# Projecting four tiles of x inside the gaps of a recurrent loop, with less room for staging, in a memory-augmented transformer with a SwiGLU gate

## The chip, the cores and the metric

The kernel runs on one core of one Trainium2 chip. The metric is the device time of one execution in microseconds (us). Times are medians of several executions. On one core the runs of one kernel differ by a few tenths of a per cent, so each experiment was timed in rounds together with the kernel before, on the same chip.

The engines have short names in the profile: PE is TensorE, PEld its weight loads, DVE is VectorE, ACT is ScalarE, POOL is GpSimd, SP is SyncE. PEclk is the clock that TensorE was granted, as a share of full speed. A number such as L354 is a line of the program of that kernel; the lines of the changed kernel are shifted against those of the kernel before.

## The reference

The forward part, cut to what matters. The kernel also computes the gradients of all nine inputs; that part is untouched.

```python
xn = layernorm(x)                          # x: (1, 2048, 640) bf16
mem = mem0                                 # (1, 8, 640)
for s in range(64):                        # segments of 32 tokens, each needs the memory of the last
    h = concat([mem, xn[:, 32*s:32*s+32]])
    q, k, v = h@Wq, h@Wk, h@Wv             # 32 heads of 128
    p = softmax(where(mask, q@k.T * 128**-0.5, -1e9))
    o = (p@v) @ Wo
    mem, out_s = o[:, :8], o[:, 8:]
g = silu( (silu(xn@w1) * (xn@w3)) @ w2 )   # SwiGLU, F = 1728
out = x + concat(out_s) * g
```

Only the 8 memory rows are recurrent. The 2048 rows of x can be projected at any time before their segment needs them.

## The kernel before

The forward part runs in this order: layer norm; SwiGLU; the turning (transposing) of the SwiGLU weights for the backward pass; the projection of the first rows of x, which also turns Wq, Wk, Wv and Wo; then the loop of 64 steps. A step is a chain: project the 8 memory rows, scores, softmax, product with v, product with Wo, next step. The other work of the loop is put into named gaps of this chain (W0, W1, W2, G1 to G6, in that order). That work is the attention of the x rows, one tile of 96 rows for every three steps, cut into eight units of four heads. Two of three steps take three units, the third takes two.

The up-front projection of 672 rows, the first seven tiles:

```python
units = wT_A_units(k, Wq, Wk_, Wv, Wo)     # 136 units: turn a piece of a weight, copy it out, store it
# pools: b0s (staging) with 3 buffers
for wi, (W, dst) in enumerate(((Wv, ...), (Wk_, ...), (Wq, ...))):
    for xt in range(6):                    # 6 x 112 rows
        for cg in range(4):
            st = stp.tile([112, 1024], BF16, name="b0st", tag="b0st")
            for b in range(2):
                ...                        # 5 matmuls 128x112 by 128x512 into pb
                k.copy(st[:, b*512:(b+1)*512], pb[:], eng='vs'[b])
            nc.sync.dma_start(dst[...], st[:])
            ...                            # then a few weight-turning units
```

The other 15 tiles cost no time of their own: 24 rows of them ride in each step, in free columns of the chain's own projection. In the gaps G2 to G5 stand seven warming matmuls of 128x512, whose results nobody reads:

```python
WARM = dict(G2=2, G3=1, G4=2, G5=2)
def gap(g):
    FILL(g, t, at, kbatch)                 # the x rows' work of this gap
    for i in range(WARM.get(g, 0)):
        nc.tensor.matmul((bA if g == "G4" else bB)[:], k.ident[:], Wq[:, 0, 0:512], start=True, stop=True)
```

The product of the x rows with v, in the gaps W0, W1 and W2, is copied to `xoT` on ScalarE and stored to DRAM as `OTX`, and ScalarE has the chain's own copies behind it:

```python
def pv(tl, qd, q=nc.gpsimd):
    ...
    ot = fl.tile([P, 4, 4, 24], BF16, name="xoT", tag="xoT", bufs=2)
    nc.scalar.copy(ot[:]..., pt[:]...)
    nc.scalar.dma_start(k.OTX[4*tl:4*tl+4, :, 4*qd:4*qd+4, :]..., ot[:]...)
```

Of the kernel before, what the change touches and what calls it, by code (L numbers as in the profile page):

```python
# [40 lines left out]
class K:  # L41
# [110 lines left out]
    def setup_dram(self):  # L152
        tc = self.tc
        S, D, T, H, F = self.S, self.D, self.T, self.H, self.F
        HD = self.HD
        dp = self.ctx.enter_context(tc.tile_pool(name="scratch", bufs=1, space=bass.MemoryType.DRAM))
        self.dp = dp
        mk = lambda name, shape, dt=BF16: dp.tile(list(shape), dt, name=name, uniquify=False)
        self.XN = mk("XN", (S, D))
        self.XNT = mk("XNT", (D, S))  # L160
        self.SLT = mk("SLT", (F, S))
        self.DUT = mk("DUT", (F, S))
        self.HB = mk("HB", (S, F))
        self.DZ = mk("DZ", (S, D))
        self.GB = mk("GB", (S, D))
        self.GS = mk("GS", (S, D))
        self.GST = mk("GST", (D, S))

        self.NR = S + 8 * T
        self.GXA = mk("GXA", (self.NR, D))  # L170
        self.HRO = mk("HRO", (self.NR, D))

        self.OT0 = 7
        self.NO = 4 * ((T - 1 - self.OT0) // 4)
        self.OTX = mk("OTX", (self.NO, P, H, 24))
        self.FS = mk("FS", (T, 64, 320))
        self.SR = mk("SR", (S, D))
        self.GWO = mk("GWO", (self.NR, D))


        self.QVS = mk("QVS", (T // 4, 4, 32, 4, 2, 1024))
        self.KS = mk("KS", (T // 4, 4, 32, 4, 1024))
        self.GOS = mk("GOS", (T // 4, 4, 32, 4, 1024))
        self.QM = mk("QM", (T, 8, HD))
        self.NB0 = 672
        self.QVX = mk("QVX", (self.NB0, 2, HD))
        self.KX = mk("KX", (self.NB0, HD))
        self.GB0 = 1344
        self.GX0 = mk("GX0", (S - self.GB0, HD))
        self.OR = mk("OR", (self.NTL * 120, HD))  # L190
        self.PR, self.DSR, self.VTD = [], [], []
        self.GXP = mk("GXP", (self.NTL, P, 8, 3, 2, 32), F32)
        for tl in range(self.NTL):
            n = self.geo(tl)[3]
            self.PR.append(mk(f"PR{tl}", (n, H, n)))
            self.DSR.append(mk(f"DSR{tl}", (n, H, n)))
            ns, nm = self.geo(tl)[0:2]
            self.VTD.append(mk(f"VTD{tl}", (P, ns, H, 40)))
        self.PM = mk("PM", (T, P, 80))
        self.WQT = mk("WQT", (HD, D))  # L200
        self.WKT = mk("WKT", (HD, D))
        self.WVT = mk("WVT", (HD, D))
        self.WOT = mk("WOT", (D, HD))
        self.W1T = mk("W1T", (F, D))
        self.W3T = mk("W3T", (F, D))
        self.W2T = mk("W2T", (D, F))
# [18 lines left out]
    def tok_src(self, x0, nx, w, c0, c1):  # L225
        if x0 + nx <= self.NB0:
            X0 = self.KX[:, c0:c1] if w == "k" else self.QVX[:, :, c0:c1] if w == "qv" else self.QVX[:, "qv".index(w), c0:c1]
            return [(0, nx, X0[x0:x0 + nx])]
        b, r = divmod(x0 - self.NB0, 96)
        assert r + nx <= 96  # L230
        return [(0, nx, self.blk_src(w, b, r, r + nx, c0, c1))]
# [174 lines left out]
def phase3_Afwd(k, W4, Wv):  # L406
    nc, tc = k.nc, k.tc
    D, DC, S, H, HD, T = k.D, k.DC, k.S, k.H, k.HD, k.T
    Wk_ = W4.tile([P, DC, HD], BF16, name="Wk", tag="w1")
# [4 lines left out]
    with tc.tile_pool(name="b0", bufs=1) as io, tc.tile_pool(name="b0s", bufs=3) as stp, \  # L414
# [5 lines left out]
        nc.sync.dma_start(Wk_[:], k.A_Wk.rearrange("(dc p) h e -> p dc (h e)", p=P))  # L420
        for wi, (W, dst) in enumerate(((Wv, k.QVX[:, 1]), (Wk_, k.KX[:, :]), (Wq, k.QVX[:, 0]))):
            for xt in range(6):
                x0 = 112 * xt
                if xt == 4 and wi == 0:
                    nc.scalar.dma_start(Wq[:], k.A_Wq.rearrange("(dc p) h e -> p dc (h e)", p=P))
                if xt == 4 and wi == 1:
                    nc.scalar.dma_start(Wo[:], k.A_Wo.rearrange("h e d -> e h d"))
                for cg in range(4):
                    st = stp.tile([112, 1024], BF16, name="b0st", tag="b0st")
                    for b in range(2):  # L430
                        c0 = cg * 1024 + b * 512
                        pb = ps.tile([112, 512], F32, name="b0pb", tag="b0pb")
                        for dc in range(DC):
                            nc.tensor.matmul(pb[:], xs[:, dc, x0:x0 + 112], W[:, dc, c0:c0 + 512],
                                             start=(dc == 0), stop=(dc == DC - 1))
                        k.copy(st[:, b * 512:(b + 1) * 512], pb[:], eng='vs'[b])
                    nc.sync.dma_start(dst[x0:x0 + 112, cg * 1024:(cg + 1) * 1024], st[:])
                    nu = ((wi * 24 + 4 * xt + cg + 1) * len(units)) // 72
# [4 lines left out]
    with tc.tile_pool(name="ast", bufs=1) as st, tc.tile_pool(name="achain", bufs=1) as ch, \  # L443
# [19 lines left out]
        rides = {}  # L463
        WARM = dict(G2=2, G3=1, G4=2, G5=2)

        def ride_ld(t):
            x0 = k.NB0 + 24 * t
            b, sub = t // 4, t % 4
            if sub == 0 and x0 < S:
# [19 lines left out]
        def ride(t):  # L489
            b, sub = t // 4, t % 4  # L490
            if k.NB0 + 96 * b >= S:
                return
# [3 lines left out]
        def chain(t, gap):  # L496
# [31 lines left out]
            qmT = ch.tile([P, H, 8], BF16, name="qmT", tag="qmT")  # L528
# [15 lines left out]
            sTm = ch.tile([40, 2, P], BF16, name="sTm", tag="sTm")  # L544
# [11 lines left out]
            sb = ch.tile([P, 2, 40], F32, name="msb", tag="msb")  # L556
# [14 lines left out]
            PTm = ch.tile([104, 8, 16], BF16, name="PTm", tag="PTm")  # L571
# [123 lines left out]
        def pv(tl, qd, q=nc.gpsimd):  # L695
# [3 lines left out]
            if 4 * tl < k.NO:  # L699
# [3 lines left out]
                ot = fl.tile([P, 4, 4, 24], BF16, name="xoT", tag="xoT", bufs=2)  # L703
# [25 lines left out]
        def gap_of(t):  # L729
# [5 lines left out]
            def gap(g):  # L735
                FILL(g, t, at, kbatch)
                m = len(batch.get(t, ()))
# [76 lines left out]
def phase3b_out(k, Wo, W0, W4):  # L814
# [8 lines left out]
    for (nm_, src, tag) in (("v", k.WVT, "w1"), ("k", k.WKT, "w2")):  # L823
        WT[nm_] = W4.tile([P, H, D], BF16, name=f"W{nm_}T", tag=tag)
# [738 lines left out]
def emit_wT_B(k: K, w1s, w3s, w2s, ps, ps_tag):  # L1563
    nc, tc = k.nc, k.tc
    D, DC, F, FC = k.D, k.DC, k.F, k.FC
    fszs = [min(P, F - fc * P) for fc in range(FC)]
    gi = 0
    with tc.tile_pool(name="wTB_st", bufs=4) as stp:
        for (nat, dstT) in ((w1s, k.W1T), (w3s, k.W3T)):
            for fc in range(FC):  # L1570
                fsz = fszs[fc]
                pt = ps.tile([P, DC, P], BF16, name="wTpt1", tag=ps_tag[gi % len(ps_tag)])
                for dc in range(DC):
                    nc.tensor.transpose(pt[0:fsz, dc, :], nat[:, dc, fc * P:fc * P + fsz], k.ident[:])
                st = stp.tile([P, DC, P], BF16, name="wTst1", tag="wTst1")
                k.copy(st[0:fsz], pt[0:fsz], eng=('v' if gi % 2 == 0 else 's'))
                gi += 1
                nc.sync.dma_start(dstT[fc * P:fc * P + fsz, :].rearrange("p (dc q) -> p dc q", q=P), st[0:fsz])
        for dc in range(DC):
            for fg in range(0, FC, 8):  # L1580
                nfc = min(8, FC - fg)
                pt = ps.tile([P, 8, P], BF16, name="wTpt2", tag=ps_tag[gi % len(ps_tag)])
                for i in range(nfc):
                    fc = fg + i
                    fsz = fszs[fc]
                    nc.tensor.transpose(pt[:, i, 0:fsz], w2s[0:fsz, fc, dc * P:(dc + 1) * P], k.ident[0:fsz, 0:fsz])
                st = stp.tile([P, 8, P], BF16, name="wTst2", tag="wTst8")
                nfull = sum(1 for i in range(nfc) if fszs[fg + i] == P)
                if nfull > 0:
                    k.copy(st[:, 0:nfull, :], pt[:, 0:nfull, :], eng=('v' if gi % 2 == 0 else 's'))  # L1590
                    gi += 1
                    nc.sync.dma_start(k.W2T[dc * P:(dc + 1) * P, fg * P:(fg + nfull) * P].rearrange("p (g q) -> p g q", q=P), st[:, 0:nfull, :])
                for i in range(nfull, nfc):
                    fc = fg + i
                    fsz = fszs[fc]
                    k.copy(st[:, i, 0:fsz], pt[:, i, 0:fsz], eng='s')
                    nc.sync.dma_start(k.W2T[dc * P:(dc + 1) * P, fc * P:fc * P + fsz], st[:, i, 0:fsz])


# [36 lines left out]
def phase2_Bfwd(k: K, Wv):  # L1636
# [5 lines left out]
    with tc.tile_pool(name="bw", bufs=1) as wp, tc.tile_pool(name="bio", bufs=2) as io, \  # L1642
            tc.tile_pool(name="bwork", bufs=2) as wk, tc.tile_pool(name="bps", bufs=2, space=bass.MemoryType.PSUM) as ps, \
# [10 lines left out]
        k.x_rows(k.HRO, k.XN, nc.gpsimd)  # L1654
        for blk in range(NBLK):
            b0 = blk * BLK
# [27 lines left out]
            for ti in range(BLK // P):  # L1684
# [33 lines left out]
                hb_tok = wk.tile([P, F], BF16, name="hb_tok", tag="hb_tok")  # L1718
# [4 lines left out]
        emit_wT_B(k, w1s, w3s, w2s, ps1, ("pht", "pz"))  # L1723
# [142 lines left out]
def kernel(  # L1866
# [35 lines left out]
    with tc.tile_pool(name="W0", bufs=1) as W0:  # L1902
        Wv = W0.tile([P, k.DC, k.HD], BF16, name="Wv", tag="w0")
        phase2_Bfwd(k, Wv)
        with tc.tile_pool(name="W4", bufs=1) as W4:
            Wo = phase3_Afwd(k, W4, Wv)
# [40 lines left out]
```

## Time and profile before

The time is 5646.7 us (median of three runs, 5643.7 to 5655.1). Times below are from the start of the profiled run, which took 5660.5 us.

| stretch | us | what holds it |
|---|---|---|
| layer norm and SwiGLU, to its last matmul | 0 to 312.5 | TensorE and the evictions |
| turns of the SwiGLU weights | 312.5 to 378.4 | evictions waiting for stores |
| up-front projection, with 136 weight-turning units | 378.4 to 593.3 | TensorE, later part |
| loop, first K matmul of step 0 to that of step 63 | 618.2 to 1908.1 (1289.9) | the recurrent chain |
| all the rest | 3751 | not touched |

The lines that carry this are shown in the prediction. To read a step one follows the chain through the engines: which instruction starts the moment another ends. A busy share does not tell it.

### The profile page before, as it was taken

The page shows a single profiled execution, that of the slowest core. Times are in us where ns is not written, and L with a number is a line of the kernel's source. Part 1 is how long each engine was busy: PE and PEld are TensorE (multiplying, and loading weights), DVE is VectorE, ACT ScalarE, POOL GpSimd, SP SyncE. Part 2 cuts the span into 40 slices and gives each one's busy share as a digit, 9 for nine tenths or more (in the row PEclk, how much of TensorE's full clock was granted, in tenths as well). Part 3 has the DMA queues.
Part 4 walks back from the last instruction along what each step waited for, and adds up shares of the span by engine and source line. Part 5 has one row for each costly group of instructions (what it writes and reads, how often), then busy time and mean ns, then how long its engine had stood idle before and what let it go on. Part 6 is the DMA issues. An engine that isn't in the chain of part 4 may idle for free. (4 is left out here: it accounts for less than half of the span.)

```text
span 5658.8 us, 167048 instructions
## 1 busy us (share of the span) xinstructions
PE 5027.7 (89%) x67614; PEld 3200.0 (57%) x67614; DVE 2387.2 (42%) x7479; ACT 1835.1 (32%) x5045; POOL 1552.1 (27%) x2576
## 2 busy tenths in 40 slices
PE   5959799999999784999999997999999999999999
PEld 2536455555555453565555554665566556657565
DVE  5824355555555423444444442332233223311451
ACT  2424355555555522333333331332223222301111
POOL 0000144444444302333333332332234223300000
PEclk9969899999999795999999998999999999999999
DMA  6465355555555475666666664543344434446332
GB/s 227 160 246 198 110 155 161 157 158 161 157 152 148 112 206 152 178 178 176 184 172 176 174 174 114 129 98 96 81 112 101 99 88 103 120 162 227 102 118 91
DMA packets 1009115, 835.82 MB, mean 148 GB/s; under 512 B 506463, under 2 KB 895875, under 8 KB 1005029
## 3 DMA queue, kind: packets, MB, share of 16 engines
q1 hardware_dynamic: 759999, 574.71, 36.2%
q0 software_dynamic: 90352, 141.70, 9.0%
q10 hardware_dynamic: 157993, 108.73, 6.7%
q8 instruction: 533, 8.73, 0.7%
q14 instruction: 238, 1.94, 0.1%
HBM read 511.81 MB, written 324.39 MB: 148 GB/s over the span
## 5 line engine op out<-in xcount | busy, mean ns | idle before, releaser
L1409 PE MATMUL wg<-gr,hr 120*128 120x512 bf16 (+1 forms) x2640 | 589.3, 384 | 17.5 <-DVE dST L1341 13.0
L1387 PE MATMUL g<-w,gT 128*128 128x320 bf16 x3840 | 549.3, 300 | 0.0
L1409 PEld LDWEIGHTS <-hr 120*128 120x128 bf16 (+1 forms) x2640 | 258.1, 99 | 340.7 <-issue 47.6
L1387 PEld LDWEIGHTS <-gT 128*128 128x128 bf16 x3840 | 369.2, 98 | 136.9
L250 POOL DMA_DIRECT2D r<-GOS x256 | 143.3, 564 | 790.3 <-PE r6p L1351 752.2
L373 PEld LDWEIGHTS <-gkv 128*8 128x8 bf16 x8192 | 213.6, 98 | 155.7 <-DVE gkv L1048 35.0
L90 DVE CAST wgo<-wg 128x512 bf16<-128x512 f32 x72 | 47.5, 687 | 584.5 <-PE wg L1409 293.5
L354 PEld LDWEIGHTS <-hx 128*32 128x32 bf16 x7680 | 178.4, 97 | 165.8 <-issue 6.6
L90 DVE CAST stg<-bank 128x512 bf16<-128x512 f32 x256 | 177.0, 691 | 202.6 <-PE bank L354 188.0
L373 PE MATMUL gbank<-WvT,gkv 128*8 128x320 bf16 x4096 | 228.7, 400 | 28.0 <-DVE gkv L1048 28.0
L663 ACT ACTIVATE xP<-xsp,xnm 120x120 bf16<-120x120 f32 (+1 forms) x704 | 239.9, 375 | 10.3 <-DVE xnm L659 5.2
L1396 DVE TENSOR_TENSOR ghacc<-ghacc,g 128x320 f32<-128x320 f32 x240 | 117.1, 488 | 277.0 <-PE g L1387 277.0
L92 ACT CAST wgo<-wg 128x512 bf16<-128x512 f32 x48 | 25.8, 589 | 637.2 <-PE wg L1409 637.2
L1354 ACT CAST gr<-r6p 120x512 bf16<-120x512 f32 (+1 forms) x176 | 103.1, 586 | 352.9 <-PE r6p L1351 340.3
L1185 POOL DMA_DIRECT2D DSR<-gdS x176 | 100.9, 573 | 410.3 <-DVE gdS L1183 382.0
L92 ACT COPY gT<-t6g 128x960 bf16<-128x960 bf16 (+5 forms) x216 | 166.8, 792 | 127.2 <-PE t6g L1370 126.7
L712 POOL DMA_DIRECT2D OR<-xv x163 | 94.7, 581 | 407.6 <-ACT xv L711 288.0
L674 POOL TENSOR_TENSOR xP<-xP,xrz 120x480 bf16<-120x480 bf16 x163 | 161.7, 992 | 140.1 <-ACT xP L663 93.4
L1183 DVE SCALAR_TENSOR_TENSOR gdS<-gdp,Dx,gPr 120x120 bf16<-120x120 f32 (+1 forms) x704 | 188.7, 330 | 0.0
L1180 DVE CUSTOM_DVE_ANT_0 gdS<-gdp,gPr 120x120 bf16<-120x120 f32 (+1 forms) x704 | 153.5, 273 | 66.3 <-PE gdp L1169 56.4
L1155 POOL DMA_DIRECT2D VTD<-gvT x176 | 129.5, 740 | 176.4 <-ACT gvT L1154 151.9
L1370 PE MATMUL t6g<-ident,gr 120*128 120x120 bf16 (+1 forms) x2112 | 171.4, 220 | 3.3 <-DVE wgo L90 2.7
(340 smaller groups left out, 11210.9 us busy)
## 6 DMA issues: line engine op xcount, KB each, us to landing
QVS<-stg SPq DMA_DIRECT2D x128, 256.0 KB
gqv<-QVS SPq DMA_DIRECT2D x112, 192.0 KB
vTt<-VTD SPq DMA_DIRECT2D x64, 320.0 KB
VTD<-gvT POOLq DMA_DIRECT2D x168, 120.0 KB, 3.4
OR<-xv POOLq DMA_DIRECT2D x163, 120.0 KB, 2.5
DSR<-gdS POOLq DMA_DIRECT2D x168, 112.5 KB, 3.3
dS<-DSR SPq DMA_DIRECT2D x168, 112.5 KB
P<-PR SPq DMA_DIRECT2D x168, 112.5 KB
```

The lines of the kernel that those rows point to most:

```text
L90: return nc.vector.tensor_copy(out, in_)
L92: return nc.scalar.copy(out, in_)
L250: eng.dma_start(d, src if src.shape[0] > 1 else src[0])
L354: k.nc.tensor.matmul(bank[32 * g:32 * g + 32, :], x[:, dc, :], W[:, dc, c0:c0 + 512], start=(dc == 0), stop=(dc == k.DC - 1), tile_positio ...
L373: k.nc.tensor.matmul(pm[p0:p0 + nq, 0:320], x[:, h, :], W[:, h, 320 * b:320 * b + 320], start=(first and i == 0), stop=(last and i == 15), ...
L663: nc.scalar.activation(Pb[0:n, j, 0:n], sp[0:n, j, :], ACT.Exp, bias=nmx[0:n, j:j + 1], scale=k.scale, accum_out=Z[0:n, j:j + 1])
L674: eng.tensor_tensor(Pb[0:n, :, 0:n], Pb[0:n, :, 0:n], bc_last(rz[0:n], n), ALU.mult)
L1180: nc.vector.tensor_tensor_reduce(dS[0:n, j, :], dp[0:n, j, :], Pr[0:n, j, :], 1.0, 0.0, ALU.mult, ALU.add, Dx[0:n, j:j + 1])
L1183: nc.vector.scalar_tensor_tensor(dS[0:n, j, :], dp[0:n, j, :], Dx[0:n, j:j + 1], Pr[0:n, j, :], op0=ALU.subtract, op1=ALU.mult)
L1370: nc.tensor.transpose(pt[:, i - i0, j, :], st["g", u, i][0:n, j * P:(j + 1) * P], k.ident[0:n, 0:n])
L1387: nc.tensor.matmul(pg[:], ring[:, i, j, r0:r0 + P], Ws[qd][i][:, j, 320 * h:320 * h + 320], start=(i == 0 and j == 0), stop=(i == 2 and j ...
L1409: nc.tensor.matmul(accs[dc][:], hr[0:n, tl, dc * P:(dc + 1) * P], st["g", NTL * qd + tl, i][0:n, :], start=(tl == 0), stop=(tl == NTL - 1))
```

## The change

The intent is to take 78 us of matmuls out of the front. Only three tiles (288 rows) are projected up front. Fifteen tiles still ride. The four tiles left (5, 9, 13 and 17) are projected in the gaps: in each of steps 4 to 51, ten real matmuls of 128x96 by 128x512 stand where the seven warming ones stood. The turning of the SwiGLU weights is moved into the last block of SwiGLU. To make room in the on-chip memory some tiles lose their second buffer, or share one.

```diff
-        self.NB0 = 672
+        self.NB0 = 288
+        self.PT = (5, 9, 13, 17)
 ... up-front projection: tiles of 96 rows, Wq and Wo fetched in nine pieces, Wk loaded earlier
+        PIECE = dict(G2=((0, 0), (0, 1), (0, 2),), G3=((0, 3), (0, 4),), G4=((1, 0), (1, 1),), G5=((1, 2), (1, 3), (1, 4),))
+        psteps = {3 * tl - 11 + i: (tl, i) for tl in k.PT for i in range(12)}
+        def piece(t, g):
+            ...
+                if dc == 0:
+                    pst["p"] = ps.tile([96, 512], F32, name="ppb", tag="x", bufs=5)
+                nc.tensor.matmul(pst["p"][:], pst["x"][:, dc, :], W[:, dc, c0:c0 + 512], ...)
+        def piece_out(t, h):
+            sg = fl.tile([96, 512], BF16, name="pst", tag="pst")
+            k.copy(sg[:], pst["p"][:], eng='vs'[h])
+            (nc.gpsimd, nc.sync)[h].dma_start(..., sg[:])
 ... qmT and msb share a buffer with fup, sTm and PTm with fsum
-                ot = fl.tile([P, 4, 4, 24], BF16, name="xoT", tag="xoT", bufs=2)
+                ot = fl.tile([P, 4, 4, 24], BF16, name="xoT", tag="xoT", bufs=1)
 ...
             def gap(g):
+                if t in psteps:
+                    piece(t, g)
+                    FILL(g, t, at, kbatch)
+                    if g in ("G3", "G5"):
+                        piece_out(t, (g == "G5") * 1)
+                    ...
+                    return
                 FILL(g, t, at, kbatch)
 ... SwiGLU: turning units after each 128 rows of the last block, hb_tok one buffer, turned weights two
```

## The prediction

> **What bounds the kernel now.** The change touches the program up to the end of the forward loop, so I cut the span into stages first: windows of busy time, one line per stage (length, then busy us and count of PE, PE's weight loads, DVE, ACT and POOL, granted clock, DMA share, GB/s).
>
> ```profile
> 63.00:98.00 35.00, 18.18 (x65) 7.23 (x64) 12.14 (x26) 7.55 (x13) 2.24 (x3) 0.78 0.68 263
> 255.00:316.00 61.00, 49.92 (x305) 27.70 (x303) 37.71 (x76) 21.18 (x33) 0.00 (x0) 0.91 0.39 127
> 317.00:360.00 43.00, 23.49 (x200) 19.36 (x199) 9.36 (x17) 12.97 (x23) 1.19 (x2) 0.55 0.57 202
> 360.00:378.30 18.30, 1.94 (x20) 1.65 (x20) 0.49 (x1) 1.43 (x3) 0.00 (x0) 0.57 0.88 338
> 378.30:465.50 87.20, 71.69 (x446) 45.54 (x447) 26.19 (x45) 26.86 (x45) 0.00 (x0) 0.88 0.75 269
> 465.50:593.00 127.50, 126.91 (x896) 83.92 (x894) 54.14 (x94) 54.16 (x94) 0.00 (x0) 1.00 0.58 194
> 618.00:1908.00 1290.00, 1191.86 (x22187) 717.52 (x22184) 736.50 (x2152) 696.28 (x2385) 550.93 (x780) 0.99 0.54 151
> ```
>
> 317 to 360 is the turning of the SwiGLU weights by itself; 378.3 to 593 the up-front projection of 672 rows (its first weight, Wv, lasts to 465.5); 618 to 1908 the 63 chained steps of the forward loop, 20.5 us each. Everything after 1908 keeps its work. The projection's second part is PE-bound (126.9 of 127.5 us busy). Its first part and the two lines above it are not; the waits from 317 to 470 say why:
>
> ```profile
> ACT wTst L92 <- DMA WVT<-wTst: 22.5, 5, 11.3
> DVE b0st L90 <- DMA QVX<-b0st: 16.6, 2, 9.5
> DVE wTst L90 <- DMA W1T<-wTst: 15.9, 1, 15.9
> ACT wTst L92 <- DMA W1T<-wTst: 14.8, 1, 14.8
> ```
>
> Evictions wait for their staging buffer's store: once for 15 us while the copy GWO<-GS runs, and then while Wk, Wq and Wo (5.2 MB each) come in.
>
> For the loop I read one step in order of time, ACT and DVE rows of step 22, a step with three softmax units (two steps of three are such; the third has two).
>
> ```profile
> 1080.74 0.86 ACT L616 COPY kT<-kpt 128x384 bf16<-128x384 bf16 x2 [0.34 <-PE kpt L614]
> 1081.52 0.53 ACT L573 COPY PTm<-bank 40x128 bf16<-40x128 bf16 x2
> 1082.07 0.36 ACT L663 ACTIVATE xP<-xsp,xnm 120x120 bf16<-120x120 f32 x1
> ...
> 1086.02 0.26 ACT L663 ACTIVATION_READ_ACCUMULATOR xP<-xsp,xnm 120x1 f32 x1
> 1086.31 0.29 ACT L384 COPY fup<-bank 64x160 f32<-64x160 f32 x1
> 1082.51 0.17 DVE L659 TENSOR_SCALAR xnm<-xmx 120x4 f32<-120x4 f32 x1
> 1082.78 0.29 DVE L581 CAST oTm<-bank 128x128 bf16<-128x128 f32 x1
> ```
>
> The recurrent chain goes through PTm, oTm, the Wo product, fup. PE is 92% busy in the loop but not the bound: it waits inside every step. In a three-unit step ACT is: twelve exps run without a gap from 1082.07, and fup follows at once, though the Wo product ended 0.64 us earlier. So any delay of PTm moves the step one for one. In a two-unit step PE's Wo product ends last, and it starts when DVE has copied oTm, which stands directly behind xnm: DVE has no slack there.
>
> **The Trainium skill.** "TensorE: Matmul & The Clock Gate", Back-to-back issue gap: the isolated warm gap is N/2.4 + 2.5 ns, 216 at N=512, and it gives 131 ns as sustained rate. The trace agrees with the first only: 216 ns start to start in the projection, 60 ns for its transposes. "DMA: Bandwidth & Descriptors", Queues, rings and completion order: each DMA engine goes round-robin between queues. The trace agrees: from 72 to 82 us PE stood 10.1 us on a 128 KB store of sl while HRO and Wv were copied by the software queue. Same page, Anatomy of one DMA: about 2 us fixed cost. Here, in the DMA packets of the trace, a 160 KB store's last packet ends about 1.7 us after its issue on a quiet queue. "Perfetto Trace Analysis", Identifying Performance Opportunities: the same gap repeating can mean too few buffers; I use it below for staging tiles the change cuts.
>
> **The change part by part.** The instruction order of both programs was compared.
>
> *Removed.* 672 rows in 6x3x4x2x5 = 720 matmuls become 288 rows in 3x3x4x2x5 = 360. 360 x 0.216 = 77.8 us of PE leave a stage that PE bounds for most of its length. Its 136 weight-turning units (about 640 transposes) stay.
>
> *New bound there.* Units per projection slot double, from 1.9 to 3.8, on three staging tiles. One tile turns in about 0.6 us copy + 0.35 issue + 1.7 landing + 0.2 = 2.9 us, so a unit per 0.97 us and 3.7 us per slot, where PE needs 10 x 0.216 + 18 x 0.06 = 3.2 us. The order shows 24 of the 32 Wv units hoisted ahead of the first projection matmul. So: 8 slots at 2.5 = 20 us, 28 at 3.7 = 103, and some 14 us of stalls while Wq and Wo (10.5 MB instead of 15.7) arrive: 137 us in place of 214.7.
>
> *Before it.* Wk's load now stands directly behind Wv's on the software queue, without a wait, so it runs at about 95 to 112 us, inside SwiGLU block 0, not block 1. Between 83 and 98 us PE did three chunks where DVE's rate (2.6 us a chunk) allows nearly six; Wk should cost 8 or 9 us. The SwiGLU turns: 15 of 38 units stand inside the last block, which should lengthen it by some 8 us (they share DVE and ACT with the block's own chain); 23 come after it. They have two staging tiles instead of four of each kind, so 1.45 us a unit, 33 us, with the Wv units in their shadow, plus the same 15 us behind GWO<-GS. First projection matmul: 312.5 + 17 + 48 = 378, where it is now. What was serial comes back as buffer waits; what is gained is that Wv units are done. The stage ends near 515 instead of 593: gain 78.
>
> *Added in the loop.* In 48 steps (4 to 51) ten real matmuls replace seven warming ones: +3 x 0.216 = 0.65 us of PE, all in gaps. That would be nearly free. But:
> 1. The DVE eviction of the first half (0.69 us) stands between xnm and oTm. Two-unit step: oTm, Wo, fup +0.62.
> 2. The half accumulator takes one of five rotating PSUM buffers through scores and kprep. In three-unit steps the second kpt now waits for ACT's copy of the first (before it waited for PE alone). Steps like 22: three matmuls first (+0.65), scores end 13.2 us into the step, kpt and its copy to 14.0, second kpt to 14.4, Pm's transpose at 14.2 instead of 13.4, PTm at 14.8 instead of 13.7: +1.1 on the ACT-bound chain. In the other three-unit steps PE has 0.7 us spare there: PTm +0.33.
> Mean (0.62 + 1.1 + 0.33)/3 = 0.68 us x 48 = 33 us.
> 3. xoT goes from two buffers to one, on ACT. By the packets, the OTX store (192-byte packets) ends 2.4 us after issue in the median and up to 4.9, and in 31 of 111 cases after the next xoT copy began. Mean wait 0.3 to 0.8 us on the second unit of a step; in steps with a third, part reaches sTm. About 0.38 us x 42 steps = 16 us.
> The ACT eviction of the second half, the two stores a step and the loads lie in idle time.
>
> Sum: -78 + 33 + 16 = -29 us, from 5647: 5618. I allow a little for the front stalls being shorter, as loads now come in pieces: 5612.
>
> **Rivals.**
> - The gaps absorb the pieces (PE fill only, +3 matmuls where it idled): loop +5 to +10 and front -80: about 5575. For it: PE's gaps of 0.3 to 0.7 us per step. Against it: DVE's copy and the kpt wait stand in the program's order.
> - The front is bound by DMA: some 34 MB in the shortened projection at the 225 GB/s of now is 150 us, not 137, and with Wk's stall the gain shrinks to 50 or less; with the loop's cost the time stays at 5640 to 5655. For it: a share of 1.0 around 370 to 400. Against it: 400 GB/s moved there.
> - Turns fully hidden in the last block and no buffer waits: front gain 110 to 120, time 5550 to 5580. For it: the block's PE idles 11 of 61 us; against it: 23 units come after it.
> - The loop's stalls chain (xoT late, then sTm, then kpt): loop +70 to +90 and nothing gained, 5640 to 5660.
>
> **Range and chances.** Front gain 55 to 105, loop cost 20 to 70, largely independent: 5570 to 5650 eight times in ten. Faster by over 2% (under 5534) needs the whole front gain and a loop that gains too: 0.02. Slower by over 2% needs 140 us more in the loop, 3 us a step: 0.01. Within 2%: 0.97.
>
> **What would show it.** Projection stage about 137 us long and no longer PE-bound, wTst evictions waiting for their stores; first projection matmul near 378; a longer block 0. Loop from first K matmul to last about 1340 us instead of 1290; steps 4 to 51 longer by 0.4 to 1.5, steps 52 on unchanged; PE kpt waiting for ACT kT, oTm directly behind the pst copy, xoT waiting for OTX. The prediction is wrong if those steps stay at 20.5 us, if the projection remains PE-bound, or if a stage after the loop moves by more than 10 us.

## The result, and the profile after

The changed kernel took 5701.1 us (median of four runs, 5696.1 to 5718.7), the kernel before 5648.7 us in the same rounds. The ratio is 1.0098, with a 95% interval of 1.0073 to 1.0122. A ratio here is the mean time of one kernel's fast runs over that of the other's of the same rounds, so it is not quite the ratio of the medians quoted. The kernel got slower by 52 us, where 35 us faster was predicted. The size is within 2%, but it lies outside the predicted range, on the wrong side.

First, the stages of the changed kernel, in the view of busy time by windows. Its columns are as in the prediction: length; busy us and count of PE, PEld, DVE, ACT, POOL; granted clock; DMA share; GB/s.

```profile
255.00:286.00 31.00, 31.00 (x171) 15.29 (x170) 27.68 (x59) 15.01 (x26) 0.00 (x0) 1.00 0.51 166
286.00:380.00 94.00, 55.75 (x532) 42.57 (x530) 32.59 (x64) 30.87 (x46) 1.19 (x2) 0.77 0.64 220
380.80:500.00 119.20, 107.83 (x750) 66.01 (x750) 42.20 (x76) 46.01 (x76) 0.00 (x0) 0.97 0.70 238
500.00:528.50 28.50, 15.95 (x120) 11.75 (x119) 6.36 (x15) 9.77 (x17) 0.00 (x0) 0.58 0.43 147
551.90:1957.50 1405.60, 1281.75 (x22329) 773.23 (x22327) 763.58 (x2200) 719.49 (x2434) 576.58 (x828) 0.94 0.52 146
```

The front did its part. The projection starts at 380.8 instead of 378.4 and ends at 528.3 instead of 593.3; the loop starts 66.3 us earlier. The loop, the last line, is 115.7 us longer (1405.6 for 1289.9). The rest of the kernel was 12 us shorter in this pair of profiled runs. That sums to -66.3 + 115.7 - 12.1 = +37.3 us between the two profiled runs; the medians differ by 52.

The last line shows something that the prediction had no step for: the granted clock is 0.94, where the loop before had 0.99.

The steps tell where in the loop it lies. Steps 0 to 3 are as long as before, and those from 52 on no longer (20.3 us in the mean, 20.6 before). Steps 46 to 51, which have pieces but no `xoT` any more, are 0.8 us longer in the mean. The rest is in steps 4 to 45, where `xoT` is written. There the waits name it; the view of waits in the loop lists engine, line, what was waited for, us in total, times, and the longest. First the kernel before, then the changed one:

```profile
ACT xoT L704 <- PE xot L702: 146.9, 84, 2.0
```

```profile
ACT xoT L741 <- DMA OTX<-xoT: 115.7, 50, 4.8
ACT xoT L741 <- PE xot L739: 82.4, 44, 3.4
...
PE kpt L651 <- ACT kT L653: 25.2, 30, 1.8
```

Before, ScalarE waited for the product only. Now, 50 of 112 copies wait for the store of the copy in front of them to have landed. Such a line counts all of the engine's idle time before the copy, also what would have been idle anyway, so 115.7 us is not what the store costs ScalarE; the net figure is in the part on waits and clock. The wait of PE kpt for ACT kT is new too, as predicted.

One step shows what such a wait sets off: step 25, which starts at 1116.86 and is 26.67 us long. ScalarE's rows in order of time, with start, duration, and in brackets the idle time before:

```profile
1125.52 0.48 ACT L741 CAST xoT<-xot 128x384 bf16<-128x384 f32 x1 [4.06 <-DMA OTX<-xoT]
...
1128.18 0.48 ACT L741 CAST xoT<-xot 128x384 bf16<-128x384 f32 x1
...
1129.68 0.36 ACT L582 CAST sTm<-bank 40x256 bf16<-40x256 f32 x1
...
1134.84 0.48 ACT L653 COPY kT<-kpt 128x384 bf16<-128x384 bf16 x1 [0.57 <-PE kpt L651]
1135.22 0.53 ACT L610 COPY PTm<-bank 40x128 bf16<-40x128 bf16 x2
```

TensorE's rows of the same step, and the step cut into three windows:

```profile
1130.10 0.24 PE L590 MATMUL bank<-ident,sTm 40*128 40x40 bf16 x2 [2.13 <-ACT sTm L582]
1130.27 1.51 PE L494 MATMUL ppb<-Wq,px 128*96 128x512 bf16 x3
```

```profile
1116.86:1129.46 12.60, 11.11 (x211) 6.14 (x209) 5.77 (x15) 4.72 (x10) 3.48 (x5) 1.00 0.60 159
1129.46:1139.70 10.24, 9.03 (x105) 4.92 (x109) 5.23 (x18) 6.61 (x31) 4.35 (x8) 0.50 0.41 118
1139.70:1143.53 3.83, 3.72 (x65) 2.62 (x58) 1.60 (x6) 1.96 (x7) 3.49 (x4) 1.00 0.56 143
```

The chain's copy sTm starts at 12.82 us into the step. TensorE, which needs it, has been idle for 2.13 us, and within that idle time its clock falls to 0.50 for 10.24 us. The three piece matmuls then take 1.51 us where they take 0.85 in the same step at full clock (shown with the first experiment). PTm starts at 18.36 us into the step, so the delay has doubled on its way.

### The profile page after: what moved, and what is told of

Same layout as the page of the kernel before. It is cut to its first block, busy times and chain, and to the rows that moved or that the text cites. A ratio compares the mean times of both kernels' runs of the same rounds, so it can differ in the third digit from the quotient of the medians.

```text
span 5696.1 us, 166875 instructions
## 1 busy us (share of the span) xinstructions
PE 5043.4 (89%) x67398; PEld 3207.7 (56%) x67398; DVE 2387.9 (42%) x7491; ACT 1837.7 (32%) x5052; POOL 1578.6 (28%) x2625
## 5 line engine op out<-in xcount | busy, mean ns | idle before, releaser
L92 ACT COPY gT<-t6g 128x960 bf16<-128x960 bf16 (+5 forms) x216 | 166.9, 792 | 119.2 <-PE t6g L1416 117.5
L382 PE MATMUL bank<-Wo,oTm 128*32 128x320 bf16 x4032 | 189.8, 347 | 6.3 <-DVE oTm L618 6.2
L575 DVE COPY vt<-stg 8x512 bf16<-8x512 bf16 x512 | 163.1, 318 | 66.0 <-ACT stg L92 59.7
L382 PEld LDWEIGHTS <-oTm 128*32 128x32 bf16 x4032 | 143.8, 111 | 64.9 <-issue 35.2
```

Source lines behind the costliest of these rows:

```text
L92: return nc.scalar.copy(out, in_)
L382: k.nc.tensor.matmul(pm[p0:p0 + nq, 0:320], x[:, h, :], W[:, h, 320 * b:320 * b + 320], start=(first and i == 0), stop=(last and i == 15), ...
L575: nc.vector.tensor_copy(vt[p0:p0 + 8, c0:c0 + 512], sv[32 * g:32 * g + 8, b * 512:(b + 1) * 512])
```

## The experiments

Fourteen kernels ran; all gave a correct result. The first theory was that the single `xoT` buffer and the pieces add up, the buffer being the larger part. The rival was that the pieces carry it. When that was settled, the question became why one missing buffer costs so much.

### 1. A second xoT buffer (e1_xot2)

Simply writing `bufs=2` does not fit: the pool would need 10.69 KB per partition where 10.31 are left. The buffer of `pst` is idle in W0 to W2, so the middle unit of a step uses it.

```diff
+            xtag = "pst" if qd in (1, 4, 7) else "xoT"
-                ot = fl.tile([P, 4, 4, 24], BF16, name="xoT", tag="xoT", bufs=1)
+                ot = fl.tile([P, 4, 4, 24], BF16, name="xoT", tag=xtag)
```

> The changed kernel with a second staging buffer for xoT: the middle unit of each step writes into the pst buffer, which is idle then, so no room is added. Theory (the single xoT buffer carries most of the loop's loss, the pieces the rest): the pieces alone cost what steps 46 to 51 show, which have pieces and no xoT, 0.8 us a step, so 48 x 0.8 = 39 us; the loop (first K matmul of step 0 to that of step 63) falls from 1405.6 us to about 1330, waits of xoT for OTX from 115.7 us to under 10, the granted clock in the loop back from 0.95 to 0.99, and the time to about 5625 (5610 to 5640), faster than before. Rival (the pieces carry it, as my prediction had it: xoT is worth 16 us): loop about 1390, time about 5685.

Measured: 5627.5 us (5621.2 to 5640.8), ratio to before 0.9948 (0.9930 to 0.9966). The loop took 1333.8 us, 71.8 less than in the changed kernel, and no wait of `xoT` for OTX above the view's limit is left. The loop's window, and the rows of step 25 (it starts at 1090.23) that answer to those above:

```profile
554.00:1887.80 1333.80, 1235.57 (x22328) 752.80 (x22327) 765.28 (x2200) 723.10 (x2433) 575.39 (x828) 0.98 0.55 153
```

```profile
1101.16 0.36 ACT L582 CAST sTm<-bank 40x256 bf16<-40x256 f32 x1
...
1105.01 0.53 ACT L610 COPY PTm<-bank 40x128 bf16<-40x128 bf16 x2
```

```profile
1101.58 0.21 PE L590 MATMUL bank<-ident,sTm 40*128 40x40 bf16 x2 [0.24 <-ACT sTm L582]
1101.72 0.85 PE L494 MATMUL ppb<-Wq,px 128*96 128x512 bf16 x3
```

The same work, one buffer name apart: sTm at 10.93 instead of 12.82 us into the step, PTm at 14.78 instead of 18.36, and the step 22.11 us long instead of 26.67. TensorE's idle time in front of the transposes is 0.24 us, not 2.13. The wait was 1.9 us at sTm, but the step lost 4.6. The clock of the loop is 0.98. The version is faster than both kernels, by half a per cent against the one before.

### 2. The kernel before with one xoT buffer (e2_before_xot1)

```diff
-                ot = fl.tile([P, 4, 4, 24], BF16, name="xoT", tag="xoT", bufs=2)
+                ot = fl.tile([P, 4, 4, 24], BF16, name="xoT", tag="xoT", bufs=1)
```

> The kernel before with one thing changed: one xoT buffer in place of two. Theory (the wait for the OTX store hurts by itself, without the pieces): loop 1290 to about 1360, time 5646 to about 5715 (5700 to 5735), clock in the loop near 0.95. Rival 1 (my prediction's size): +16 us, 5662. Rival 2 (the wait only hurts where the pieces have made the step late): under +10.

Measured: 5728.1 us, ratio 1.0130 (1.0115 to 1.0145); loop 1354.1 us, 64 more than before, clock 0.95. The buffer hurts without any piece, four times as much as I had put down for it.

### 3. The four tiles projected up front, one xoT buffer (e3_front7)

```diff
-            for x0 in range(0, k.NB0, 96):
+            for it, x0 in enumerate([96 * i for i in (0, 1, 2) + k.PT]):
-        psteps = {3 * tl - 11 + i: (tl, i) for tl in k.PT for i in range(12)}
+        psteps = {3 * tl - 11 + i: (tl, i) for tl in () for i in range(12)}
 ... (loads of the four tiles' rows, count of units per slot)
```

> The changed kernel with its four piece tiles projected up front like the first three; the gaps of the loop have their warming matmuls again, xoT keeps one buffer. Theory (costs of xoT and pieces add): loop 1405.6 minus 39 = about 1366; the front takes 360 matmuls x 0.216 = 78 us more, so the time is about 5735 (5720 to 5750). Rival (the two only hurt together): loop about 1305, time about 5675. Rival (pieces carry it all): loop about 1306 too, but then e1 stays near 5685.

Measured: 5742.9 us, ratio 1.0157 (1.0138 to 1.0176); loop 1376.8 us. The costs add, roughly: without pieces the loop is 29 us shorter than in the changed kernel, and it is 87 longer than before. It is also 23 us longer than e2, whose loop should be nearly the same; that is taken up in 6.

### 4. The DVE eviction moved behind oTm (e4_xot2_late)

On top of e1:

```diff
+                    if g == "G4":
+                        piece_out(t, 0)
                     piece(t, g)
                     FILL(g, t, at, kbatch)
-                    if g in ("G3", "G5"):
-                        piece_out(t, (g == "G5") * 1)
+                    if g == "G5":
+                        piece_out(t, 1)
```

> e1, and the DVE eviction of the first half of a piece (pst, 0.69 us) is issued after the two oTm copies instead of in front of them. Theory (the eviction stands in the recurrent chain, 0.62 us in two-unit steps and some of it in the others): 48 steps x 0.2 to 0.6, so 10 to 28 us less than e1, about 5605. Rival (the pieces cost through the PSUM buffers and PE time, not through DVE): within 5 us of e1.

Measured: 5643.9 us, ratio 0.9980 (0.9960 to 0.9999), slower than e1 by 16 us; loop 1341.0. A miss. In two-unit steps the next memory rows (hx) came 0.33 us earlier, as expected, but the step was as long as in e1, 20.78 for 20.77 us in the median. In step 26 the trace shows GpSimd's normalisation of a softmax unit behind the later store of `pst` on its queue, and TensorE's last transposes waiting for it. In three-unit steps the eviction now stands in front of the third unit's row maximum. Number 10 tests the first of these two.

### 5. The piece behind the K transposes (e5_xot2_g2)

On top of e1:

```diff
-                    piece(t, g)
+                    if g != "G2":
+                        piece(t, g)
                     FILL(g, t, at, kbatch)
+                    if g == "G2":
+                        piece(t, g)
```

> e1 (second xoT buffer), and the three piece matmuls of the gap before Pm's transpose stand behind that gap's scores and K transposes instead of in front of them, so that the half accumulator takes its PSUM buffer after both K transposes had theirs. Theory (in one three-unit step of three the second K transpose waits for ScalarE's copy of the first, which puts Pm's transpose 1.1 us late): there Pm's transpose comes 0.4 us late instead of 1.0, in the other steps it moves by 0 to +0.3; loop 1333.8 to about 1325, time about 5618 (5608 to 5628). Rival (PE's own time is the limit there, wherever the three matmuls stand): loop within 4 us of 1334.

Measured: 5618.0 us, ratio 0.9933 (0.9914 to 0.9953); loop 1322.0 us, 11.8 less than e1. The waits of PE kpt for ACT kT, 15.6 us in e1's loop, are gone, and the three-unit steps concerned fell from 22.18 to 21.83 us in the median. As expected, within 3 us.

### 6. No pieces, two xoT buffers (e6_front7_xot2)

The edits of 1 and 3 together.

> No pieces in the loop (their tiles projected up front) and the second xoT buffer: only the shared buffers of qmT, msb, sTm and PTm are left of what the change does to the loop. Theory (those cost nothing, and e3 was 23 us longer in the loop than e2 by the luck of landing times): loop 1290 to 1296, time about 5650. Rival (the shared buffers cost some 20 us): loop about 1312, time about 5670; then pieces alone are worth only some 22 of e1's 44.

Measured: 5651.8 us, ratio 0.9997 (0.9973 to 1.0021); loop 1292.6 us, for 1289.9 before. So the shared buffers of qmT, msb, sTm and PTm cost at most 3 us, and the pieces alone 1333.8 - 1292.6 = 41 us. The 23 us between e2 and e3 don't come from those buffers as long as nothing is late. What they come from is not shown by a run of its own; the table below shows that e3 had 24 steps with a halved clock and e2 19.

### 7. OTX stored in larger packets (e7_otx768)

In the changed kernel, one buffer kept; a store writes 768 bytes per partition in one piece.

```diff
-        self.OTX = mk("OTX", (self.NO, P, H, 24))
+        self.OTX = mk("OTX", (self.NO // 4, 8, P, 4, 4 * 24))
 ... (the load reads the same bytes in pieces of 192)
```

> The changed kernel with its one xoT buffer, but OTX laid out so that a store writes 768 bytes in one piece per partition in place of four of 192 (the load of it then reads pieces of 192). Theory A (the store is late because of its 512 small packets): waits of xoT for OTX fall from 115.7 to under 60 us, loop 1405 to about 1370, time about 5665. Theory B (its fixed cost and the other traffic make it late): waits stay above 95 us, loop above 1390, time above 5685.

Measured: 5693.4 us, ratio 1.0071 (1.0046 to 1.0095); waits 97.0 us in 41 places; loop 1380.9. The waits and the time are where theory B had them, the loop 9 us below its limit. Where a copy waited, the time from the issue of the store to the start of that copy was 3.7 us in the median, as in the changed kernel. The packet size is not the main reason why the store is late.

### 8. Six staging buffers in the projection (e8_b0s6)

On top of e1:

```diff
-            tc.tile_pool(name="b0s", bufs=3) as stp
+            tc.tile_pool(name="b0s", bufs=6) as stp
```

> e1 with six staging buffers instead of three in the up-front projection. Theory (the stage, 148 us, is held by evictions waiting for their staging tile's store, most of all in its last 27 us, which are Wo's turns alone): stage 148 to about 125, time about 5605. Rival (the loads of Wq and Wo and PE's order of work hold it): within 6 us of e1.

Measured: 5596.0 us, ratio 0.9894 (0.9874 to 0.9913). The stage took 110.9 us (384.7 to 495.6) instead of 148.8, more than expected. The last stretch, from the first of Wo's turns to the end, first e1, then e8:

```profile
493.20:529.20 36.00, 25.66 (x191) 17.68 (x190) 10.33 (x23) 13.17 (x23) 0.00 (x0) 0.69 0.49 165
```

```profile
464.00:495.60 31.60, 30.89 (x257) 20.50 (x256) 14.94 (x29) 16.14 (x30) 0.00 (x0) 1.00 0.68 225
```

With three buffers PE is busy 25.7 of 36 us at a clock of 0.69; with six it is busy 30.9 of 31.6 us at 1.00 and does a third more matmuls (257 for 191). Over the whole stage PE is now busy 107.9 of 110.9 us, so it is PE's own time that is left; most of the 38 us above it were waits for staging tiles.

### 9. Warming matmuls where TensorE idles (e9_warm_g1)

In the changed kernel, one buffer kept:

```diff
                     FILL(g, t, at, kbatch)
+                    for i in range(3 if g == "G1" else 0):
+                        nc.tensor.matmul(bA[:], k.ident[:], Wq[:, 0, 0:512], start=True, stop=True)
```

> The changed kernel with its one xoT buffer kept, and three warming matmuls (128x512, 0.65 us) added to TensorE in each of the 48 steps, between the first scores and the transpose of sTm, where TensorE stands idle while ScalarE waits for the OTX store. What it tests: in the changed kernel 22 of the 42 steps with xoT have the granted clock at half for 3.4 to 10.2 us after that idle time, and these 22 are 64 of the 72 us that the single buffer costs; the other 20 cost 8 us. Theory (the wait itself is cheap, its price is the clock that falls after TensorE idled 0.7 to 2.7 us): the dips mostly go, the clock in the loop rises from 0.95 to 0.98 or more, the loop falls from 1405.6 to about 1355 (the added matmuls cost 0.4 us in steps that do not wait, some 10 us of it), time about 5650. Rival (the wait is what costs): waits of xoT for OTX and the loop stay as they are, within 10 us of 1406, or get 20 us longer by the added matmuls.

Measured: 5686.5 us, ratio 1.0063 (1.0046 to 1.0079); loop 1396.2, 9 us less, with 31 us of matmuls added: steps 46 to 51, which have no wait, got 0.65 us longer each, not 0.4 as I had expected. The waits of `xoT` are still 108.6 us. The clock lost in steps 4 to 45 (the time at half clock, halved) fell from 68 to 32 us. So the dips (stretches at half clock) did not all go, and the expected loop of 1355 us was missed. By its letter the rival came true: the waits nearly stayed, and the loop is within 10 us of 1406. What speaks against it is that matmuls which cost 0.65 us in a step without a wait made the loop no longer.

### 10. Late eviction in two-unit steps only (e10_two_late)

On top of e5:

```diff
-                    if g in ("G3", "G5"):
-                        piece_out(t, (g == "G5") * 1)
+                    if g == ("G4" if t % 3 == 2 else "G3"):
+                        piece_out(t, 0)
+                    if g == "G5":
+                        piece_out(t, 1)
 ... (one accumulator per half; the store of the first half on SyncE's queue in these steps)
```

> e5, and in two-unit steps alone the first half of a piece is evicted at the end of the gap behind the oTm copies, after the reciprocals of the softmax units, with its store on the SyncE queue. e4 moved it in all steps and gained nothing: hx came 0.33 us earlier in two-unit steps, but the store on GpSimd's queue now stood in front of GpSimd's normalisation, and TensorE waited for that before the next step. Theory (that is why e4 failed): two-unit steps fall from 20.75 to 20.3, 16 x 0.4 = 7 us in all: loop 1322 to about 1315, time about 5611. Rival (the two-unit step is held by something else, TensorE's pieces for one): loop within 3 us of 1322.

Measured: 5606.5 us, ratio 0.9924 (0.9900 to 0.9948), which does not differ from e5's 0.9933; loop 1321.9. The two-unit steps fell to 20.31 us in the median, as expected, so the explanation of e4 holds for them. The loop did not gain: the two-unit steps are 4.8 us shorter in sum than in e5, but the steps right after them 4.0 longer, and those from 52 on, which the edit does not touch, 2.7. A likely reason stands in the waits in the loop, first e5, then e10:

```profile
ACT pst L92 <- DMA QVX<-pst: 0.7, 2, 0.4
```

```profile
ACT pst L92 <- DMA QVX<-pst: 21.1, 12, 3.7
```

Both halves of a piece share one staging buffer. The first half is now evicted late in two-unit steps, so the second waits for its store, mostly into the next step. If that is what held the loop, which no run tests, it is the error of the change once more.

### 11 and 12. The parts together (e11_best, e12_wst3)

e11 is e10 with the six staging buffers of e8. e12 also gives the turned SwiGLU weights three staging buffers instead of two.

> The parts that helped, together: second xoT buffer, the three piece matmuls behind the K transposes, six staging buffers in the projection, the late eviction in two-unit steps. If they add: 5596 (e8) minus 10 (e5) minus 7 (e10) = about 5580 (5570 to 5592), against about 5650 of before: faster than both kernels. If the loop's starting time matters or they overlap: 5590 to 5600.

> e11 with three staging buffers instead of two for the turned SwiGLU weights in the last block of the first phase. Theory (these evictions wait for their stores between the last block's end and the projection, also once for 14 us behind the copy of the gates): the projection's first matmul comes 5 to 12 us earlier than the 384.7 us of e8, time about 5572. Rival (the loads and that copy hold this stretch, not the buffers): within 4 us of e11.

Measured: e11 5584.7 us, ratio 0.9882 (0.9861 to 0.9902); e12 5576.9 us, ratio 0.9858 (0.9826 to 0.9890). Both beat the kernel before and the changed one. In e12 the projection's first matmul came 21 us earlier than in e11 (362.7 for 384.0), where 5 to 12 was expected, but the loop started only 6.6 us earlier. The intervals of the two overlap, so that e12 is the better one is not shown.

### 13. The piece moved into the idle place (e13_piece_g1)

In the changed kernel, one buffer kept. No matmul is added: the three of G2 stand in G1, behind its fill.

```diff
-        PIECE = dict(G2=((0, 0), (0, 1), (0, 2),), ...
+        PIECE = dict(G1=((0, 0), (0, 1), (0, 2),), ...
```

> The changed kernel with its one xoT buffer; the three piece matmuls of the gap before Pm's transpose stand one gap earlier, in front of the transpose of sTm, where TensorE idles behind the OTX wait. Number of matmuls, buffers and waits as in the changed kernel. Theory (the halved clock after that idle time carries most of the loss): dips fall to half or less, lost clock in steps 4 to 45 from 68 us to 35 or less, the loop from 1405.6 to about 1370 (1360 to 1380; in steps without a wait the transpose comes 0.4 us later, which eats some), time about 5662. Rival (the wait itself): xoT waits some 110 us as before and loop 1395 to 1410, time 5690 to 5705.

Measured: 5687.3 us, ratio 1.0068 (1.0051 to 1.0085); waits 126.2 us, more than the changed kernel's 115.7; loop 1385.6, 20 us less; lost clock 43 us. That is a good half of what was expected, between the theory and the rival. The place that the matmuls left is now idle itself: in two-unit steps TensorE waits 0.8 us for Pm, and dips start behind it.

### 14. No warming matmuls in the kernel before (e14_before_nowarm)

```diff
-        WARM = dict(G2=2, G3=1, G4=2, G5=2)
+        WARM = dict()
```

> The kernel before without the seven warming matmuls of each step; nothing else. TensorE then idles in several gaps of a step, each under 1.5 us by what the steps show, and no xoT wait is there. Theory (idle times of 0.7 us and more[...] are enough to halve the clock): clock in the loop from 1.00 to 0.9 or less, loop 1290 to 1330 or more. Rival (it takes longer idle times): clock stays over 0.97 and the loop stays within 10 us or gets shorter.

Measured: 5730.1 us, ratio 1.0139 (1.0124 to 1.0154). The loop:

```profile
617.30:1985.20 1367.90, 1188.37 (x21743) 778.80 (x21742) 736.11 (x2152) 696.83 (x2385) 551.22 (x780) 0.90 0.51 142
```

441 matmuls fewer, and the loop is 78 us longer, with the clock at 0.90. No idle time of TensorE in steps 4 to 45 was longer than 1.16 us.

### Waits and clock together

Steps 4 to 45, each kernel against a twin without the wait (in e14: with the warming matmuls). The changed kernel, e2 and e3 differ from their twin in the one buffer alone; e7, e9 and e13 also in their own edit. "Lost clock" is the time at half clock, halved. A step counts as a dip if it lost over 0.5 us more clock than the same step of the twin.

| kernel, twin | longer by, us | waits for OTX, us | lost clock, us (twin) | dip steps: n, longer by | other steps: n, longer by |
|---|---|---|---|---|---|
| changed, e1 | 72.1 | 115.7 | 68.3 (8.5) | 22, 63.9 | 20, 8.2 |
| e2, before | 62.4 | 101.4 | 54.6 (1.7) | 19, 56.0 | 23, 6.4 |
| e3, e6 | 82.7 | 96.3 | 70.0 (5.1) | 24, 76.2 | 18, 6.4 |
| e7, e1 | 47.9 | 97.0 | 46.1 (8.5) | 14, 40.5 | 28, 7.3 |
| e13, e1 | 48.8 | 126.2 | 42.7 (8.5) | 17, 41.8 | 25, 7.0 |
| e9, e1 | 57.9 | 108.6 | 32.4 (8.5) | 10, 35.2 | 32, 22.7 |
| e14, before | 57.8 | none | 93.9 (1.7) | 37, 57.3 | 5, 0.5 |

Nearly all of the loss sits in the dip steps, 2.5 to 3.5 us each where there are waits. Part of that is the wait itself, since the waits were longer there: over steps 4 to 45 ScalarE's idle time in front of the `xoT` copies, whatever ended it, grew from 150.6 us in e1 to 213.5 in the changed kernel, 42 us of it in the dip steps and 21 in the others. How much of it got into the chain is seen at sTm. TensorE's wait for it in the loop, first the changed kernel, then e1:

```profile
PE bank L590 <- ACT sTm L582: 42.9, 34, 2.7
```

```profile
PE bank L590 <- ACT sTm L582: 14.0, 31, 1.6
```

Counted from the start of each step, sTm came 29.3 us later in sum than in e1, 21.8 of it in the dip steps. The steps got 72.1 us longer. So 43 us arose behind sTm, and 42 of them in the 22 dip steps; behind sTm the other 20 steps lost 0.7 us together. e2 against before gives the same picture: 25.3 us at sTm, 62.4 in all. A few of the 42 us are K transposes that came late in steps where sTm did not; the rest goes with the halved clock.

e14 has the dips without the waits: 92 us of clock lost beyond its twin and 57 us longer in the dip steps, 1.5 us each. At that rate, 0.6 us for each us of clock lost, the 60 us that the changed kernel lost beyond its twin would be worth 37; that is an estimate. e13 has more waits than the changed kernel, fewer dips, and a smaller loss. In e9, 0.65 x 32 = 20.8 of the 22.7 us are the added matmuls.

Lengths and dips come from one profiled execution of each kernel. The clock itself is no luck of one profile: over the whole kernel it was 0.929 to 0.932 in all four timed runs of the changed kernel, 0.941 to 0.943 in those of e1, and 0.920 to 0.923 in those of e14. But in each trace the dips begin on one grid of 3.41 us (all 27 of steps 4 to 45 in the changed kernel, all 42 in e14), so where the idle times fall against that grid matters too, and single steps should not be compared between runs.

## Why the prediction was wrong

**The change part by part, point 3: "About 0.38 us x 42 steps = 16 us." This step failed.** The buffer cost 72 us (the changed kernel against e1) or 64 (e2 against before). It was mis-sized in two ways.

The first is the landing. I took the end of the last packet, 2.4 us after issue in the median, as the moment when the buffer is free. Before the change the next copy came 2.7 to 2.9 us after the store's issue in all 70 pairs within one step, so 31 of 111 copies (28%) looked late, by 20 us in sum. In the changed kernel 50 of the 70 copies that follow another within a step waited, and they started 2.3 to 5.9 us after that issue, 3.7 in the median. For the 50 stores that they waited for, the last packet ended 3.0 us after issue in the median, and the semaphore came 0.64 us after it (0.33 to 1.06). With 0.64 us added to each store of the trace before, 52 of the 111 copies are late, by 44 us in sum. The Trainium skill knows this part: "DMA: Bandwidth & Descriptors", Anatomy of one DMA, written for the software queue, puts most of a fixed cost of about 2 us into the receipt of the write, which comes after the last byte and before the semaphore. The trace agrees on the order; on this hardware queue the part was smaller, 0.64 us. So the wait that reached sTm was 29 us, 0.70 us a step and not 0.38.

The second is larger: the clock. What I had no term for is that TensorE, idle for 0.7 to 2.7 us in front of most dips, behind the late sTm or a late K transpose, was given half clock for 3.4 to 10.2 us, in the middle of the recurrent chain. In step 25 the wait put sTm 1.9 us late and the step 4.6. Over all steps that is the other 43 us, for the most part. The seven warming matmuls in the kernel before were there to be read, and I read them as filler that pieces replace. e14 shows what they were worth, 78 us.

**Points 1 and 2, the pieces: right.** I had +1.1 us in the three-unit steps with a second K transpose behind a copy, +0.33 in the other three-unit steps, and +0.62 in two-unit steps. e1 against before shows +1.19, +0.37 and +0.64 in the medians of steps 4 to 45. The sum was 33 us; e6 and e1 give 41; the rest lies in single steps, some with a dip (10, 34, 40) and some without (22, 49). The mechanisms were shown by undoing them. e5 took the K wait away and got 12 us. The delay of oTm by the pst copy went in two-unit steps in e10, at the price of a new wait.

**Removed and New bound there: right in kind, a little short.** The front gained 66.3 us, for 78. The first projection matmul came at 380.8, for 378. The stage took 147.5 us, for 137: its last 28 us are Wo's turns on three staging tiles, 15.95 us of PE in 28.5. I had a tile's cycle as 2.9 us, and that was right: these turns came every 0.93 us, 2.8 us for three tiles. (They took 56 ns a transpose, not 60.) What I had wrong is the overlap. I spread the turns evenly beside the projection; in the order that ran, 30 of Wo's 40 came behind the last projection matmul, with nothing else for PE to do. e8 shows that more buffers remove this stretch; the order of the instructions changed with them.

**Before it: right in the sum, with some luck.** Block 0 and Wk's load: the last gate matmul of SwiGLU came 9.5 us later, for 8 or 9. The last block with its turns: its end 11.8 us later, for 17. The turns and waits behind it took 56.5 us, for 48, so two errors nearly cancel in the time of the first projection matmul.

**What would show it.** PE kpt waits for ACT kT, steps 52 on unchanged, `xoT` waits for OTX: all came. Steps 4 to 51 were to be 0.4 to 1.5 us longer: 46 to 51 were 0.8, steps 4 to 45 were 2.7. Of my three conditions for being wrong, the first did not come about. The second did in part: PE was busy 107.8 of 119.2 us up to 500, but 15.95 of 28.5 after it. The third did. The stage after the loop moved by 12 us, more than the 10 I had allowed. In the profiled runs with the change's layout it took 3726 to 3751 us, in those without it 3748 to 3753, so a part may be real. No run tells why.

**The rivals.** The fourth, stalls that chain, was the nearest: loop +70 to +90 and 5640 to 5660. It had the right start, but nothing of the clock, and it was still too small: the loop got 116 us longer.

The sum with the measured terms: -66 (front) + 41 (pieces) + 72 (buffer) = +47 us, where the medians differ by 52. With the second buffer it is -25, and e1 measured -28.

## What to carry to other kernels

Before taking a second buffer away, compare the time until its next use with the time until the store's semaphore comes, not until its last packet. A margin of half a microsecond at the median was none here. Then ask which engine will stand idle behind that wait: if it is TensorE in a chain that just keeps its clock, allow for several microseconds at half clock behind the idle time. Before dummy matmuls in a tuned kernel are replaced, take them out in a run of their own and see what they are worth. Room can often be had without memory, by lending a buffer that is idle in that part of the step.

## What the Trainium skill lacked or had wrong

- "TensorE: Matmul & The Clock Gate", Why this matters for your kernels: it gives gaps of more than about 3 us between bursts as what throws the clock back, one idle window. Here the clock was halved with far shorter idle times. In e14 none in steps 4 to 45 was over 1.16 us, and 37 of 42 steps had a dip. In the changed kernel an idle time of 0.7 to 2.7 us stood in front of 23 of 27 dips. Another section of the page, A second HAM failure mode, does tell of frequent short idle times that make the clock swing, but gives no length. The dips lasted 3.41, 6.83 or 10.24 us and began on a grid of 3.41 us, which agrees with the page's free-running window of 3413 ns.
- Same page, Back-to-back issue gap: the sustained rate of 131 ns a matmul at N=512 was not seen; 216 ns start to start was in the projection.
- "DMA: Bandwidth & Descriptors", Anatomy of one DMA: its fit for the software queue, with a constant fixed cost of about 2 us, gives 2.2 us for 96 KB (an estimate). The stores of 96 KB on the hardware queue that were waited for took 3.6 us to the semaphore in the median and up to 5.9, and packets of 768 instead of 192 bytes did not change the median. Only 0.64 us of that lay behind the last packet.
- No page that I read says how much margin a single staging buffer needs beside other traffic. In e2, where the copies follow as in the kernel before, 2.7 to 2.9 us were not enough in 49 of 70 cases.
